# Loading the first x tile alone and transposing the second by DMA in a gated attention/SwiGLU kernel

## The chip, the cores and the metric

The kernel runs on one core of a Trainium2 chip. The metric is the device time of one execution in microseconds (us). The core's engines run side by side: PE (the tensor engine: matmuls, and weight loads shown as PEld), DVE (vector), ACT (scalar), POOL (GpSimd) and SP (sync, which here only issues DMAs). Work on different engines is ordered by semaphores.

## The reference

x has 2048 rows of 512 bf16 values. Two blocks read the same x, and a gate per row mixes them:

```python
g = _sigmoid((x * gate_w).sum(-1, keepdims=True))
a = _A_ref(x, A_wqkv, A_wo)     # linear attention, 32 heads of 16
b = _B_ref(x, B_w1, B_w3, B_w2) # silu(x w1) * (x w3), then w2; inner width 1376
return g * a + (1 - g) * b
```

In block A, `phi(t) = where(t > 0, t + 1, exp(t)) + 1e-6` is applied to q and k; `kv` is the sum over all rows of phi(k) times v per head, `z` the sum of phi(k), and the output is `(phi(q) kv) / (phi(q) z)` times `wo`.

## The kernel before

Rows are worked in 16 tiles of 128 (`t`), the inner dimension of 512 in 4 chunks of 128 (`kc`). Two forms of x are kept on the chip: `xN`, with a row per partition (the natural rows), and `xT`, with a column of x per partition, which the projections need as the stationary operand.

There are two stages. In the first, for each tile, k = x wk and q = x wq are computed (four matmuls of 512 columns each, L169), phi is applied by ACT and DVE, and G, the product of x transposed and phi(k), is summed over all tiles in four PSUM banks (`g_step`, L217), so that v never has to be formed. POOL sums phi(k) for z. In the second stage the SwiGLU matmuls run in blocks of 512 rows, with attention's remaining steps and the output in between. Schedule and queues are written out by hand: each engine runs its instructions in the order of the program.

Nearly all loads are issued by SP on one queue, in the order of the program: the natural rows of tiles 0 and 1 together (L119, 256 KB, with two neighbouring rows of x on one partition, so that "tile 0" holds the even rows of the first 256), the four pieces of wq and wk (`load_wqk`, L116, one piece of 256 KB per `kc`), x tile by tile in transposed form by a transposing DMA for tiles 2 to 15 (`load_xT`, L113), with natural rows in between (L131: tiles 2 and 3 after x tile 3, tiles 4 to 7 after 5, tiles 8 to 15 after 8), and then the other weights. `touch` (L123) is a small load on ACT's queue.

Tiles 0 and 1 get their xT on the tensor engine: `transpose_block` (L323) multiplies a block of xN by the identity into PSUM, and DVE or ACT copies it to xT (L337 to L340, L352). Before that, `warm_step` (L317) runs matmuls on constants. The order on the tensor engine at the start is: 13 warm steps; transposes of chunks 0, 1 and 2 of both tiles (6); the projections of both tiles for kc 0 in the order k0, q0, k1, q1; the 2 transposes of chunk 3; the four projections for kc 1; then k of both tiles for kc 2 and 3, q of tile 0 and of tile 1 for kc 2 and 3, k of tile 2, and three of the four chunks of G of tile 0. Because row pairs were loaded for tiles 0 and 1, their output rows are stored with a stride of two rows.

Of the kernel before, what the change touches and what calls it, by code (L numbers as in the profile page):

```python
# [8 lines left out]
ACT = mybir.ActivationFunctionType  # L9
# [7 lines left out]
def kernel(  # L17
# [17 lines left out]
    nc = tc.nc  # L35
    P = nc.NUM_PARTITIONS
# [5 lines left out]
    KC = D // P  # L42
# [11 lines left out]
    x2d = A_x.flatten_outer_dims()  # L54
    out2d = out.flatten_outer_dims()
# [19 lines left out]
        out=bmask[:], in_=bmask[:], pattern=[[-Dh, HPC], [0, Dh]], compare_op=ALU.is_ge,  # L75
# [3 lines left out]
        out=bmask[:], in_=bmask[:], pattern=[[Dh, HPC], [0, Dh]], compare_op=ALU.is_ge,  # L79
# [17 lines left out]
    xN = consts.tile([P, NT, D], BF16, name="xN")  # L97
# [9 lines left out]
    xT = consts.tile([P, KC, S], BF16, name="xT")  # L107
    act_pre = consts.tile([P, 1], BF16, name="act_pre")
    dq = nc.sync

    def load_xT(t):
        ts = slice(t * P, (t + 1) * P)
        dq.dma_start(out=xT[:, :, ts], in_=x2d[ts, :], transpose=True)  # L113

    def load_wqk(kc):
        dq.dma_start(out=wqk[:, kc, :], in_=wqkv_r[:, kc, 0 : 2 * D])  # L116

    x_first = x2d[0 : 2 * P, :].rearrange("(p j) d -> p j d", j=2)
    dq.dma_start(out=xN[:, 0:2, :], in_=x_first)  # L119
    nc.scalar.activation(out=act_pre[:], in_=warm[:, 0:1], func=ACT.Exp)  # L120

    touch = consts.tile([P, 2, 16], BF16, name="touch")
    nc.scalar.dma_start(out=touch[:], in_=wqkv_r[:, 1:3, 0:16])  # L123
    for kc in range(KC):
        load_wqk(kc)
    natural = {3: (2, 4), 5: (4, 8), 8: (8, 16)}
    for t in range(2, NT):
        load_xT(t)
        if t in natural:
# [2 lines left out]
    with nc.allow_non_contiguous_dma(reason="gate column"):  # L132
        dq.dma_start(
            out=wr[:, :, 2 * FR : NR], in_=gate_w.rearrange("(kc d o) -> d kc o", d=P, o=1)
# [21 lines left out]
    bank = [psum.tile([P, D], FP32, name=f"bank{i}") for i in range(8)]  # L156
    turn = {"mm": 0, "ab": 0}

    def mm_tile():
        turn["mm"] += 1  # L160
        return bank[4 + (turn["mm"] - 1) % 4]

    def ab_tile():
        turn["ab"] += 1
        return bank[(turn["ab"] - 1) % 4]
# [149 lines left out]
    def warm_step(n):  # L315
        for _ in range(n):
            nc.tensor.matmul(  # L317
                bank[7][:, 0:256], lhsT=warm[:, 0:P], rhs=warm, start=True, stop=True
            )

    def transpose_block(t, kc, dst):

        nc.tensor.matmul(  # L323
            dst, lhsT=xN[:, t, kc * P : (kc + 1) * P], rhs=ident[:], start=True, stop=True
        )

    def transpose_kc(kc, ps):
        for t in range(2):
            transpose_block(t, kc, ps[:, t * P : (t + 1) * P])

    warm_step(13)

    for t in range(2):
        transpose_block(t, 0, bank[t][:, 0:P])
    transpose_kc(1, bank[2])
    transpose_kc(2, bank[3])
    nc.vector.tensor_copy(out=xT[:, 0, 0:P], in_=bank[0][:, 0:P])  # L337
    nc.scalar.activation(out=xT[:, 0, P : 2 * P], in_=bank[1][:, 0:P], func=ACT.Copy)
    nc.vector.tensor_copy(out=xT[:, 1, 0 : 2 * P], in_=bank[2][:, 0 : 2 * P])
    nc.scalar.activation(out=xT[:, 2, 0 : 2 * P], in_=bank[3][:, 0 : 2 * P], func=ACT.Copy)  # L340
    first = {(t, n): mm_tile() for n, t in (("k", 0), ("k", 1), ("q", 0), ("q", 1))}
    w_of = {"k": wk, "q": wq}

    def first_mm(n, t, kc):
        proj_mm(first[t, n], t, w_of[n], kc)

    for kc in range(2):
        for n, t in (("k", 0), ("q", 0), ("k", 1), ("q", 1)):
            first_mm(n, t, kc)
        if kc == 0:  # L350
            transpose_kc(3, bank[0])
            nc.vector.tensor_copy(out=xT[:, 3, 0 : 2 * P], in_=bank[0][:, 0 : 2 * P])  # L352
    for kc in range(2, KC):
        for t in range(2):
            first_mm("k", t, kc)
# [67 lines left out]
    def out_step(tb, tt):  # L423
        t = tb * TPB + tt
        ts = slice(t * P, (t + 1) * P)
        tl = slice(tt * P, (tt + 1) * P)
        a_ps = ab_tile()
        for c in range(KC):
            nc.tensor.matmul(  # L429
                a_ps[:], lhsT=pqT[:, c, ts], rhs=M2[:, c, :],  # L430
                start=(c == 0), stop=(c == KC - 1),
            )
        aga = work.tile([P, D], FP32, tag="aga", name="aga")
        nc.scalar.activation(out=aga[:], in_=a_ps[:], func=ACT.Copy, scale=g_all[:, t : t + 1])  # L434
        o = work.tile([P, D], BF16, tag="o", bufs=3, name="o")
        last = t == NT - 1
        for lo, w in ((0, 2 * P), (2 * P, P), (3 * P, P)) if last else ((0, D),):
            cs = slice(lo, lo + w)
            b_ps = ab_tile()
            for fc in range(FC + 1):  # L440
                n = P if fc < FC else FR
                nc.tensor.matmul(  # L442
                    b_ps[:, 0:w], lhsT=hT[tb][:n, fc, tl], rhs=w2[:n, fc, cs],
                    start=(fc == 0), stop=(fc == FC),
                )
            nc.vector.scalar_tensor_tensor(  # L446
                out=o[:, cs], in0=b_ps[:, 0:w], scalar=omg_all[:, t : t + 1], in1=aga[:, cs],
                op0=ALU.mult, op1=ALU.add,
            )
            if t < 2:  # L450
                rows = out2d[0 : 2 * P, :].rearrange("(p j) d -> p j d", j=2)[:, t, :]
            else:
                rows = out2d[ts, :]
            if last and w == P:

                if lo + w < D:
                    continue
                cs = slice(2 * P, D)
            dq.dma_start(out=rows[:, cs], in_=o[:, cs])
# [3 lines left out]
    for tb in range(NTB):  # L463
        for fc in range(FC):
            glu_step(tb, fc)
            if tb == 0:
                if fc in den_at:
                    den_step(den_at[fc])
                if fc == 2:
                    kv_step()  # L470
                if fc == 4:
                    m2_step()
                    z_order()
                    den_products(0)
                if fc == 7:
                    rem_step(0)
        for tt in range(TPB):
            out_step(tb, tt)
            if tb + 1 < NTB:
                if tt == 0:  # L480
                    hT[tb + 1] = work.tile([P, FC + 1, TB], BF16, tag="hT", name="hT")
                if tt == 1:
                    rem_step(tb + 1)
                den_step((tb + 1) * TPB + tt)
# [30 lines left out]
```

## Time and profile before

| what | value |
|---|---|
| median of 3 runs | 179.36 us (178.71 to 179.49) |
| profiled execution, span from first to last instruction | 177.9 us |
| the median less that span | about 1.4 us |
| PE busy | 174.3 us (98%) |
| DVE / ACT / POOL busy | 101.5 / 62.2 / 63.5 us |
| transposes on PE (L323) | 8 matmuls, 6 from 3.74 us and 2 from 6.17 us |
| first projection (L169) starts | 4.51 us |

The profiled execution's time is known by its span; what lies around the span is taken from the difference to the runs. A row of the timeline names the start, the length, the engine, the line, the operation, the tile written and the tile read, and in brackets how long the engine was idle before it and what ended that. SPq is SP issuing a DMA: the length is that of the issue, not of the transfer. Matmuls are pipelined and their ends are modelled, so the distance between starts tells more than the lengths.

### The profile page before, as it was taken

The numbers are of one execution on the slowest core, as the hardware profiler recorded it, in microseconds if no ns is written. First come the engines' busy times: TensorE is split into PE (matmuls) and PEld (weight loads), VectorE is DVE, ScalarE is ACT, GpSimd is POOL, SyncE is SP. The second block draws the span as 40 slices with busy tenths as digits, with TensorE's granted clock in tenths as the row PEclk, the third lists the DMA queues.
The fourth block names the chain that finished last, engine by engine and source line by source line (L and its number), as shares of the span: only waits on it lengthen the run. The fifth ranks groups of instructions, "written<-read, shape, count | busy, mean of one in ns | idle before, by whom it ended". The sixth has DMA issues, their size and how long they took to land.

```text
span 177.9 us, 2504 instructions
## 1 busy us (share of the span) xinstructions
PE 174.3 (98%) x879; PEld 84.1 (47%) x879; DVE 101.5 (57%) x195; ACT 62.2 (35%) x113; POOL 63.5 (36%) x105
## 2 busy tenths in 40 slices
PE   8999999999999999999999999999999999999993
PEld 5444444444454464644444464444445444444453
DVE  0299798888865888666344166634325564333222
ACT  3255444544744332331333223242321223342130
POOL 5077667557301676846300044540004432000000
DMA  6978959993103025243100013520000342000001
GB/s 175 266 209 233 168 100 315 391 350 111 33 0 29 0 55 66 66 95 106 29 0 4 0 33 85 94 57 4 0 0 29 88 92 59 0 0 0 29 33 59
DMA packets 29724, 15.41 MB, mean 87 GB/s; under 512 B 21552, under 2 KB 28048, under 8 KB 29712
## 3 DMA queue, kind: packets, MB, share of 16 engines
q1 hardware_dynamic: 29440, 15.25, 35.2%
q8 instruction: 7, 0.11, 0.3%
q10 hardware_dynamic: 272, 0.01, 0.1%
q14 instruction: 5, 0.04, 0.1%
HBM read 8.56 MB, written 2.10 MB: 60 GB/s over the span
## 4 chain that ended last, share of the span: by engine, by line
PE 98%; DVE 0%; issue 0%
PE bank L442 21%; PE bank L264 19%; PE bank L270 19%; PE bank L169 16%; PE bank L429 8%; PE bank L217 8%; PE bank L231 3%; PE bank L317 2%; PE bank L323 1%; PE bank L404 1%; PE bank L417 0%; DVE o L446 0%
## 5 line engine op out<-in xcount | busy, mean ns | idle before, releaser
L276 DVE TENSOR_TENSOR hT<-bank,sg 128x512 bf16<-128x512 f32 x40 | 27.3, 682 | 32.4 <-PE bank L270 32.4
L264 PE MATMUL bank<-xT,w 128*128 128x512 bf16 x160 | 41.1, 379 | 0.0
L270 PE MATMUL bank<-xT,w 128*128 128x512 bf16 x160 | 41.1, 379 | 0.0
L442 PE MATMUL bank<-w,hT 128*128 128x512 bf16 (+3 forms) x198 | 40.7, 355 | 0.0
L275 ACT ACTIVATE sg<-bank 128x512 bf16<-128x512 f32 x40 | 23.9, 597 | 46.7 <-PE bank L264 46.7
L298 POOL TENSOR_TENSOR pqs<-pq,rden 128x512 bf16<-128x512 bf16 x16 | 16.9, 1056 | 55.7 <-issue 48.2
L169 PE MATMUL bank<-wqk,xT 128*128 128x512 bf16 x128 | 31.2, 386 | 0.0
L442 PEld LDWEIGHTS <-hT 128*128 128x128 bf16 (+1 forms) x198 | 18.5, 98 | 19.8
L446 DVE SCALAR_TENSOR_TENSOR o<-bank,omg_all,aga 128x512 bf16<-128x512 f32 (+2 forms) x18 | 12.4, 692 | 25.6 <-PE bank L442 25.5
L201 POOL TENSOR_TENSOR zacc<-zacc,pk 128x128 f32<-128x128 f32 x56 | 23.3, 446 | 10.4 <-DVE pk L187 10.4
L270 PEld LDWEIGHTS <-w 128*128 128x128 bf16 x160 | 15.7, 98 | 18.9
L264 PEld LDWEIGHTS <-w 128*128 128x128 bf16 x160 | 15.6, 98 | 18.4
L434 ACT ACTIVATE aga<-bank,g_all 128x512 f32<-128x512 f32 x16 | 11.0, 688 | 28.9 <-PE bank L429 28.9
L169 PEld LDWEIGHTS <-xT 128*128 128x128 bf16 x128 | 12.6, 99 | 15.1 <-issue 0.6
L283 POOL TENSOR_TENSOR pr<-pq,zb 128x512 f32<-128x512 bf16 x16 | 18.5, 1156 | 0.1
L217 PE MATMUL bank<-pk,xN 128*128 128x512 bf16 x64 | 16.4, 379 | 0.0
L429 PE MATMUL bank<-M,pqT 128*128 128x512 bf16 x64 | 16.4, 378 | 0.0
L182 ACT ACTIVATE eq<-bank 128x512 bf16<-128x512 f32 x16 | 9.4, 598 | 16.0 <-PE bank L169 16.0
L187 DVE SCALAR_TENSOR_TENSOR pk<-bank,emk 128x512 bf16<-128x512 f32 x16 | 11.1, 692 | 1.6
L182 ACT ACTIVATE ek<-bank 128x512 bf16<-128x512 f32 x16 | 9.5, 597 | 7.1 <-PE bank L169 7.1
L187 DVE SCALAR_TENSOR_TENSOR pq<-bank,emq 128x512 bf16<-128x512 f32 x16 | 11.1, 692 | 0.5
L287 DVE TENSOR_REDUCE den<-pr 128x32 f32<-128x512 f32 x16 | 10.8, 676 | 0.0
(48 smaller groups left out, 82.6 us busy)
## 6 DMA issues: line engine op xcount, KB each, us to landing
w<-in_B_w_dram SPq DMA_DIRECT2D x3, 1280.0 KB, 10.1
out_dram<-o SPq DMA_DIRECT2D x15, 128.0 KB, 1.9
wqk<-in_A_wqkv_dram SPq DMA_DIRECT2D x4, 256.0 KB, 3.9
xN<-in_A_x_dram SPq DMA_DIRECT2D x1, 1024.0 KB, 5.8
xN<-in_A_x_dram SPq DMA_DIRECT2D x2, 256.0 KB, 3.1
xN<-in_A_x_dram SPq DMA_DIRECT2D x1, 512.0 KB, 3.7
wv<-in_A_wqkv_dram SPq DMA_DIRECT2D x1, 512.0 KB, 11.0
wo<-in_A_wo_dram SPq DMA_DIRECT2D x1, 512.0 KB, 12.0
```

Source lines behind the costliest of these rows:

```text
L169: nc.tensor.matmul(ps[:], lhsT=xT[:, kc, t * P : (t + 1) * P], rhs=w[:, kc, :], start=(kc == 0), stop=(kc == KC - 1),)
L182: nc.scalar.activation(out=e[:], in_=ps[:], func=ACT.Exp)
L187: nc.vector.scalar_tensor_tensor(out=dst, in0=ps[:], scalar=0.0, in1=em[:], op0=ALU.max, op1=ALU.add)
L201: nc.gpsimd.tensor_tensor(out=(zaccb if t == NT - 1 else zacc)[:, cs], in0=zacc[:, cs], in1=pk[t][:, cs], op=ALU.add,)
L217: nc.tensor.matmul(bank[kc][:], lhsT=xN[:, t, kc * P : (kc + 1) * P], rhs=pk[t][:], start=(t == 0), stop=(t == NT - 1),)
L264: nc.tensor.matmul(g_ps[:], lhsT=w1[:, kc, fs], rhs=xT[:, kc, tok], start=(kc == 0), stop=(kc == KC - 1),)
L270: nc.tensor.matmul(u_ps[:], lhsT=w3[:, kc, fs], rhs=xT[:, kc, tok], start=(kc == 0), stop=(kc == KC - 1),)
L275: nc.scalar.activation(out=sg[:], in_=g_ps[:], func=ACT.Silu)
L276: nc.vector.tensor_tensor(out=hT[tb][:, fc, :], in0=u_ps[:], in1=sg[:], op=ALU.mult)
L283: nc.gpsimd.tensor_tensor(out=pr[t][:], in0=pq[:, t, :], in1=zb[:], op=ALU.mult)
L429: nc.tensor.matmul(a_ps[:], lhsT=pqT[:, c, ts], rhs=M2[:, c, :], start=(c == 0), stop=(c == KC - 1),)
L442: nc.tensor.matmul(b_ps[:, 0:w], lhsT=hT[tb][:n, fc, tl], rhs=w2[:n, fc, cs], start=(fc == 0), stop=(fc == FC),)
```

## The change

Natural rows of tile 0 are loaded alone (128 KB). x tile 1 comes by a transposing DMA, issued on SP's queue right behind piece 0 of wq/wk and ahead of pieces 1 to 3. Its natural rows are loaded together with those of tiles 2 and 3. The tensor engine runs 12 warm steps instead of 13, transposes only the four chunks of tile 0, each copied at once by DVE or ACT, and the two transposes between kc 0 and kc 1 are gone. Tiles 0 and 1 hold plain rows now, so their stores are like all others.

```diff
-    x_first = x2d[0 : 2 * P, :].rearrange("(p j) d -> p j d", j=2)
-    dq.dma_start(out=xN[:, 0:2, :], in_=x_first)
+    dq.dma_start(out=xN[:, 0, :], in_=x2d[0:P, :])
...
     for kc in range(KC):
         load_wqk(kc)
-    natural = {3: (2, 4), 5: (4, 8), 8: (8, 16)}
+        if kc == 0:
+            load_xT(1)
+    natural = {3: (1, 4), 5: (4, 8), 8: (8, 16)}
...
-    def transpose_kc(kc, ps):
-        for t in range(2):
-            transpose_block(t, kc, ps[:, t * P : (t + 1) * P])
-
-    warm_step(13)
-
-    for t in range(2):
-        transpose_block(t, 0, bank[t][:, 0:P])
-    transpose_kc(1, bank[2])
-    transpose_kc(2, bank[3])
-    nc.vector.tensor_copy(out=xT[:, 0, 0:P], in_=bank[0][:, 0:P])
-    nc.scalar.activation(out=xT[:, 0, P : 2 * P], in_=bank[1][:, 0:P], func=ACT.Copy)
-    nc.vector.tensor_copy(out=xT[:, 1, 0 : 2 * P], in_=bank[2][:, 0 : 2 * P])
-    nc.scalar.activation(out=xT[:, 2, 0 : 2 * P], in_=bank[3][:, 0 : 2 * P], func=ACT.Copy)
+    warm_step(12)
+
+    for kc in range(KC):
+        transpose_block(0, kc, bank[kc][:, 0:P])
+        if kc % 2 == 0:
+            nc.vector.tensor_copy(out=xT[:, kc, 0:P], in_=bank[kc][:, 0:P])
+        else:
+            nc.scalar.activation(out=xT[:, kc, 0:P], in_=bank[kc][:, 0:P], func=ACT.Copy)
...
     for kc in range(2):
         for n, t in (("k", 0), ("q", 0), ("k", 1), ("q", 1)):
             first_mm(n, t, kc)
-        if kc == 0:
-            transpose_kc(3, bank[0])
-            nc.vector.tensor_copy(out=xT[:, 3, 0 : 2 * P], in_=bank[0][:, 0 : 2 * P])
...
-            if t < 2:
-                rows = out2d[0 : 2 * P, :].rearrange("(p j) d -> p j d", j=2)[:, t, :]
-            else:
-                rows = out2d[ts, :]
+            rows = out2d[ts, :]
```

## The prediction

> **What bounds the kernel now.** I read four views in this order. First the page's span, engines and chain:
>
> ```profile
> span 177.9 us, 2504 instructions
> PE 174.3 (98%) x879; PEld 84.1 (47%) x879; DVE 101.5 (57%) x195; ACT 62.2 (35%) x113; POOL 63.5 (36%) x105
> PE 98%; DVE 0%; issue 0%
> ```
>
> The chain that ends last is the tensor engine from end to end. So the change, which touches only the first ten microseconds, counts by how far it moves the point from which that engine runs without a gap: a shift there goes through to the end one for one. The page calls the engine busy nearly everywhere, so stalls must be read from starts. The timeline of the first 10 us (start, length, engine, line):
>
> ```profile
> 0.81 0.40 SPq L119 DMA_DIRECT2D xN<-in_A_x_dram  x1
> 0.84 2.93 PE L317 MATMUL bank<-const-bfloat16-1.0 128*128 128x256 bf16 x13 [0.84 <-PEq L499]
> 1.27 1.83 SPq L116 DMA_DIRECT2D wqk<-in_A_wqkv_dram  x4
> 3.14 2.60 SPq L113 DMA_TRANSPOSE xT<-in_A_x_dram  x2
> 3.74 0.82 PE L323 MATMUL bank<-ident,xN 128*128 128x128 bf16 x6
> 4.07 0.29 DVE L337 CAST xT<-bank 128x128 bf16<-128x128 f32 x1 [4.07 <-PE bank L323]
> 4.51 1.85 PE L169 MATMUL bank<-wqk,xT 128*128 128x512 bf16 x4
> 5.79 0.58 SPq L131 DMA_DIRECT2D xN<-in_A_x_dram  x1
> 6.17 0.30 PE L323 MATMUL bank<-ident,xN 128*128 128x128 bf16 x2
> 6.31 3.62 PE L169 MATMUL bank<-wqk,xT 128*128 128x512 bf16 x16
> ```
>
> Four 512-column matmuls take from 4.51 to 6.17, 0.427 apart; the next sixteen go 0.216 apart. The column of granted clock says 1.00 throughout; the spacing says half speed until about 6.2. SP spends 0.46 on a plain load but 1.3 on a transposing one. Next, the DMA view in narrow windows, one transfer at a time; the last number is us from issue to landing. In order: xN, the four pieces of wqk, x tile 2, and x tile 15, which has the queue to itself:
>
> ```profile
> xN<-in_A_x_dram SPq DMA_DIRECT2D x1, 256.0 KB, 2.9
> wqk<-in_A_wqkv_dram SPq DMA_DIRECT2D x1, 256.0 KB, 3.2
> wqk<-in_A_wqkv_dram SPq DMA_DIRECT2D x1, 256.0 KB, 3.4
> wqk<-in_A_wqkv_dram SPq DMA_DIRECT2D x1, 256.0 KB, 4.4
> wqk<-in_A_wqkv_dram SPq DMA_DIRECT2D x1, 256.0 KB, 4.6
> xT<-in_A_x_dram SPq DMA_TRANSPOSE x1, 4.7
> xT<-in_A_x_dram SPq DMA_TRANSPOSE x1, 2.6
> ```
>
> Issued at 0.81, 1.27, 1.73, 2.20, 2.67 and 3.14, these land at 3.71, 4.47, 5.13, 6.60, 7.27 and 7.84. The transposes start at 3.74 and the first projection at 4.51: each starts as its load lands. The later pieces have room: piece 1 is first used at 6.31, piece 2 at 7.17, piece 3 at 7.17+2x0.216 = 7.60, with 1.2, 0.6 and 0.3 to spare. Last, the table of stretches (columns: PE, PEld, DVE, ACT, POOL busy, clock, DMA share, GB/s) and the packets from 5.85 to 6.65:
>
> ```profile
> 3.10:5.80 2.70, 2.70 (x14) 1.27 (x12) 0.72 (x2) 0.66 (x2) 0.18 (x1) 1.00 1.03 357
> 24.00:24.40 0.40, 0.40 (x3) 0.20 (x2) 0.30 (x1) 0.37 (x1) 0.00 (x0) 1.00 1.07 248
> DMA packets 541, 0.18 MB, mean 224 GB/s; under 512 B 513, under 2 KB 513, under 8 KB 541
> ```
>
> Plain loads run at 357 GB/s, x tile 15's transposing load at 248. By 6.65 the 512 small packets of tile 2 have moved, yet piece 3, ahead of it in the queue, lands only at 7.27 and tile 2 at 7.84.
>
> **The change, part by part.** All against the profiled execution, span 177.93; the median of the runs, 179.36, lies 1.43 above it, and I carry that over unchanged.
>
> *Half the first load.* 128 KB less at 357 GB/s is 0.37: xN lands near 3.34. Twelve warm steps 0.213 apart (the thirteenth of before started at 3.36) end their slots at 3.40. Four transposes 0.107 apart (128 of the 512 columns that take 0.427) follow, to 3.83; copies take 0.29 each, two on DVE and two on ACT, starting 0.33 after the first transpose, so the first piece of xT is ready at 4.02. Transposes are off the path so far.
>
> *Piece 0 of wqk.* Its issue stays at 1.27; with 128 KB less ahead it could land at 4.47-0.37 = 4.10. But it now has a transposing load right behind it, as piece 3 had, and that one's notice came 0.6 after tile 2's packets had moved. Tile 1's packets should move from about 3.1 (its issue ends at 3.0) to 3.9, at most 4.3; so the upper end is 4.9. I take the middle, 4.5: no gain, no loss.
>
> *Tile 1 by DMA.* Issue 1.73 to 3.0. Alone such a load lands 2.6 after issue (4.33); behind the full queue 4.7 (6.43). Only 384 KB stand ahead of it, so I lean to the free row: 4.4 to 5.2. The two matmuls of tile 0 at 4.5 cover it to 4.5+2x0.427 = 5.35. Cost nothing; without that cover up to 1.1.
>
> *Two transposes and a copy between kc 0 and kc 1 go.* 6.17 to 6.31: 0.14 saved. Four cold matmuls from 4.5 end at 6.21; kc 1 starts there, 0.10 ahead of before. Piece 1 must be there: issued at 3.02 instead of 1.73, it lands at 3.02+2.9 (xN's row) = 5.9, at most 5.13+1.29 = 6.42. About covered.
>
> *Pieces 1 to 3 are issued 1.29 later.* This is the cost. Piece 3 is wanted at 6.21+6x0.216 = 7.50. Lower end: the bytes ahead are the same, only tile 1's 128 KB move at 248 instead of 357, +0.16: 7.43, no wait. Upper end: the whole 1.29, 8.56. Between: the plain load issued behind tile 5's transpose ended its issue at 9.54 and reached full rate about 10.6; piece 1, whose issue ends at 3.45, by the same step runs fully at 4.2 to 4.5, and three pieces at 0.75 each end at 6.5 to 6.8 against about 6.2 before. I take +0.5: piece 3 lands at 7.77 and kc 3 of k waits 0.27. Order on the engine keeps all q matmuls behind that wait, so all of it is on the path.
>
> One page bears on this: the Trainium skill, Advanced Engine Details and Errata, X-Bar Transpose (TRN2), says transposing DMAs are as fast as regular ones. The rows here disagree (248 against 357 GB/s, 1.3 against 0.46 of issue); by the page piece 3 would be in time and the sum -0.10.
>
> *Later rows.* Tile 1's rows move to the load after x tile 3: issue at 5.79+1.29 = 7.08, landing 3.3 later plus 0.37 for 128 KB more: 10.75; first used by G of tile 1 at 11.27 plus the shift. Covered with 0.5; without cover, the excess. x tile 2 lands at 7.84+0.5 = 8.34, at worst (1.29) 9.13, and is wanted at 8.90+0.17 = 9.07: covered, at worst 0.06 late. x tile 3 (8.3 before, at worst 9.6) is wanted at 10.41, tile 4 (10.0, 11.3) at 13.2. Everything behind on SP is 1.29 later: the last weights are issued by 37 before and first wanted past 47. The first two stores write plain rows: same bytes, no row waits on them. DVE and ACT lose three copies beside the path.
>
> Sum: -0.10 + 0.27 = +0.17, span 178.1, time 179.53; I say 179.6, since every unread term (hold, second gap) leans to later.
>
> **The rivals.**
> *A, nothing is late.* Pieces 0 and 3 land at their lower ends, 4.10 and 7.43. Then kc 0 ends at 5.81, kc 1 starts 0.4 early with one slow matmul, kc 3 waits at most 0.1: about -0.3, 179.0; if the clock also rises earlier, -0.65, 178.7. For it: equal bytes. Against it: SP's 1.3.
> *B, the queue loses the whole issue.* Piece 3 lands at 8.56 plus up to 0.3 of hold; kc 3 starts 0.95 to 1.25 later than 7.60: 180.3 to 180.6. It decides once piece 3 lands after 8.5. For it: piece 3 lands 0.6 to 1 after its packets. Against it: DMA engines, not SP, were the limit before.
> *C, the slow spell lasts longer.* The slow spacing lasted from 0.84 to 6.2, 5.4 us with gaps of 0.17 and 0.15. Now the gap between transposes and first projection is 0.3 to 1.0. If the count starts anew at 4.5, full speed comes at 9.9: from 6.21 to 9.9 there is room for 3.7/0.427 = 8.7 matmuls, each 0.211 dearer, 1.8 in all, and piece 3's wait vanishes in it: 179.36-0.10+1.83 = 181.1. It decides at a gap long enough to break the count; no row tells how long. The Trainium skill, TensorE: Matmul & The Clock Gate, Part 1, says full clock follows a busy window of about 3.4 us whose phase is free; by it a spoiled window costs about 1.7. The trace agrees on a slow start and shows nothing of the windows.
>
> **How the numbers follow.** Main course (-0.2 to +0.6, 179.2 to 180.0) 0.55; A 0.17; B 0.15; C 0.13. 0.5% is 0.9 us, about what a measurement of this kernel can tell from no change. Faster by that needs all of A and an earlier clock: 0.05. Slower by that: B and C, 0.28. Within: 0.67. The range runs from just below A's end to B's end, 178.6 to 180.8; C (0.13) and A's tail stay outside.
>
> **What would show it.** Right: transposes at 3.4, first projection about 4.5, no L323 row after kc 0, a gap of 0.2 to 0.5 on the tensor engine before kc 3 (near 7.5), piece 3 landing 7.5 to 8.0, G steps without a gap. Wrong: first projection at 4.1 and no gap (A); piece 3 after 8.5 (B); 0.427 spacing beyond 6.5 (C); a gap in front of G of tile 1 if its rows land after 11.4.

## The result, and the profile after

| | kernel before | changed kernel |
|---|---|---|
| median of 14 runs each | 179.35 us (178.70 to 179.78) | 180.05 us (179.61 to 180.33) |
| ratio to before | | 1.0041, interval 1.0029 to 1.0054 |
| profiled execution | span 177.9 | span 178.2, time 180.05 |

Medians, ranges and numbers of runs, here and below, are those of executions at the usual speed; single slower ones, of 1.5% and more above the fastest of their kernel, are left out.

The change costs 0.70 us between the medians. That is inside the prediction's 0.5%, but near its slow end and just above the main course, which ended at 180.0. The interval lies wholly above 1, so the loss is clear of the noise.

The page of the changed kernel, its span, its busy times and, from its fourth part, the chain that ended last by engine:

```profile
span 178.2 us, 2478 instructions
...
PE 172.7 (97%) x858; PEld 83.6 (47%) x874; DVE 100.9 (57%) x194; ACT 62.0 (35%) x113; POOL 63.4 (36%) x105
...
PE 94%; DMA 2%; SPq 2%; issue 1%; DVE 0%
```

PE's busy time fell by 1.6, but the 21 matmuls that are missing against the 879 of before are only in part gone (four transposes and a warm step); the others are most likely missing records: a second profile of the unchanged kernel, with 863, lacks the same 16. More telling, the chain is no longer PE alone: 2% of it is a DMA and 2% SP's issues. The chain in order of time says where (start, length, what):

```profile
1.73 1.29 SPq L113
...
3.06 0.57 SPq L116
...
3.68 0.43 SPq L116
...
4.15 3.59 DMA wqk<-in_A_wqkv_dram
7.75 0.04 issue
7.79 2.32 PE bank L170 x10
```

SP's time goes straight into the chain: the transposing load of tile 1 holds SP for 1.29, so piece 3 of wq/wk is issued at 4.15 (before: 2.67), lands at 7.75, and the tensor engine, which wanted it earlier, starts kc 3 at 7.79. From there to the end the chain is PE again. The timeline of the same stretch (start, length, engine, line; in brackets the idle time before and what ended it):

```profile
3.36 0.63 PE L324 MATMUL bank<-ident,xN 128*128 128x128 bf16 x4
4.40 1.28 PE L170 MATMUL bank<-wqk,xT 128*128 128x512 bf16 x4 [0.41 <-DMA wqk<-in_A_wqkv_dram]
5.07 0.33 PEld L170 LDWEIGHTS <-xT 128*128 128x128 bf16 x3 [0.56 <-DMA xT<-in_A_x_dram]
5.97 4.14 PE L170 MATMUL bank<-wqk,xT 128*128 128x512 bf16 x16 [0.29 <-DMA wqk<-in_A_wqkv_dram]
```

The row at 5.97 hides two more gaps, because it joins sixteen matmuls. The single starts of the 512-column matmuls, taken from the traces, show them (`|` marks a gap):

```
after    4.40 4.78 5.07 5.30 | 5.97 6.19 6.40 6.62 | 7.08 7.30 | 7.79 8.00 ...  G of tile 0 at 9.94
before   4.51 4.89 5.32 5.75 | 6.31 6.52 6.74 6.96   7.17 7.39   7.60 7.82 ...  G of tile 0 at 9.76
```

In before's row the mark stands for the two transposes there. Full speed (0.216 from start to start) came at 4.8 in this execution and at 6.2 in before's. So the tensor engine was through with each piece sooner, and waited three times, by the starts less 0.216: 0.46 before kc 1, 0.25 before kc 2, 0.28 before kc 3. It all ends where piece 3 lands. The DMA view, one transfer at a time, gives tile 1's transposing load and pieces 1, 2 and 3, in this order (the last number is us from issue to landing; the issues are at 1.73, 3.06, 3.68 and 4.15):

```profile
xT<-in_A_x_dram SPq DMA_TRANSPOSE x1, 3.3
wqk<-in_A_wqkv_dram SPq DMA_DIRECT2D x1, 256.0 KB, 2.9
wqk<-in_A_wqkv_dram SPq DMA_DIRECT2D x1, 256.0 KB, 3.4
wqk<-in_A_wqkv_dram SPq DMA_DIRECT2D x1, 256.0 KB, 3.6
```

Each piece is faster from issue to landing than before (3.4, 4.4 and 4.6 there), with less of the queue still ahead of it; but it is issued 1.33 to 1.48 later, and that is not won back in full: they land at 5.93, 7.04 and 7.75 instead of 5.13, 6.59 and 7.27. The stretch from 4.0 to 5.5 in the table of stretches, first of the changed kernel, then of the one before (last two columns: share of the DMA engines, GB/s):

```profile
4.00:5.50 1.50, 1.10 (x4) 0.42 (x5) 0.21 (x2) 0.31 (x2) 0.00 (x0) 1.00 0.83 207
```

```profile
4.00:5.50 1.50, 1.50 (x9) 0.81 (x7) 0.72 (x2) 0.66 (x2) 0.00 (x0) 1.00 1.01 348
```

The transfers that before kept the queue full run at 207 GB/s in a stretch where before moved 348. That hole goes with the later issue; whether it alone makes it is taken up below.

From about 8 us on, PE has no gap in either kernel. So the effect on the tensor engine is in the start: in the two profiled executions G of tile 0 begins at 9.76 and 9.94 (+0.18). Another 0.10 lies behind the last matmul, where the span goes on for 2.80 in before and 2.90 after. Together that is 0.28 of the 0.70. The rest is taken up below.

The 0.10 has nothing to do with the pieces. The changed kernel has one DMA more (73 against 72). At the end SP waits for the semaphores of the DMAs one after another; when the last store has landed, one such wait is left in before, and in the changed kernel the one that SP stands at and two more. The kernels of the experiments show the same: from the end of the last matmul to the end of the span it is 2.79 to 2.80 in the six traces with 72 DMAs, 2.88 to 2.90 in the seven with 73, and 3.04 in the one with 75.

### The profile page after: what moved, and what is told of

It reads as the page before. It is cut to its first block, busy times and chain, and to the rows that moved or that the text cites. A ratio compares the mean times of both kernels' runs of the same rounds, so it can differ in the third digit from the quotient of the medians.

```text
span 178.2 us, 2478 instructions
## 1 busy us (share of the span) xinstructions
PE 172.7 (97%) x858; PEld 83.6 (47%) x874; DVE 100.9 (57%) x194; ACT 62.0 (35%) x113; POOL 63.4 (36%) x105
## 4 chain that ended last, share of the span: by engine, by line
PE 94%; DMA 2%; SPq 2%; issue 1%; DVE 0%
PE bank L434 21%; PE bank L265 20%; PE bank L271 19%; PE bank L170 14%; PE bank L421 8%; PE bank L218 8%; PE bank L232 3%; DMA wqk<-in_A_wqkv_dram 2%; SPq L116 1%; SPq L113 1%; PE bank L396 1%; PE bank L409 0%; SPq L118 0%; DVE o L438 0%
## 5 line engine op out<-in xcount | busy, mean ns | idle before, releaser
L265 PE MATMUL bank<-xT,w 128*128 128x512 bf16 x158 | 41.0, 379 | 0.3
L434 PE MATMUL bank<-w,hT 128*128 128x512 bf16 (+4 forms) x197 | 40.6, 355 | 0.1
L271 PE MATMUL bank<-xT,w 128*128 128x512 bf16 x154 | 40.3, 379 | 0.2
```

What stands on the lines that cost most here:

```text
L265: nc.tensor.matmul(g_ps[:], lhsT=w1[:, kc, fs], rhs=xT[:, kc, tok], start=(kc == 0), stop=(kc == KC - 1),)
L271: nc.tensor.matmul(u_ps[:], lhsT=w3[:, kc, fs], rhs=xT[:, kc, tok], start=(kc == 0), stop=(kc == KC - 1),)
L434: nc.tensor.matmul(b_ps[:, 0:w], lhsT=hT[tb][:n, fc, tl], rhs=w2[:n, fc, cs], start=(fc == 0), stop=(fc == FC),)
```

## The experiments

The theory on which the expectations rest ("Theory 1" in some of them): the pieces are issued late because SP spends 1.29 on a transposing load, and the tensor engine waits for them; the profiled execution of before stands above its own median, so the loss seen against it is too small. The rivals: the place of the transposing load in the queue, not SP's time, holds the pieces; the gaps keep the matmul clock low for longer; or something else in the start than the pieces. Medians are given with the number of runs; the kernel before, run beside them in three groups, had 179.34, 179.44 and 179.32 us.

| kernel | median us (range, runs) | ratio, interval | KB moved by 5.5 us | piece 3 lands |
|---|---|---|---|---|
| before, again | 179.35 (178.74-179.96, 12) | 1.0004 [0.9988, 1.0020] | 1108 | 7.22 |
| before, a third time | 179.53 (1) | | 1122 | 6.76 |
| before, plain rows behind piece 3 | 179.33 (178.79-179.78, 12) | 0.9992 [0.9978, 1.0006] | 1094 | 6.61 |
| before, first load split | 179.80 (179.19-181.49, 12) | 1.0036 [1.0012, 1.0060] | 906 | 7.37 |
| before, one tiny load | 180.06 (179.59-180.50, 7) | 1.0038 [1.0022, 1.0054] | 856 | 7.23 |
| before, three tiny loads | 180.09 (179.80-180.28, 12) | 1.0031 [1.0018, 1.0043] | 816 | 7.48 |
| before, wk first | 180.24 (179.72-181.80, 10) | 1.0064 [1.0037, 1.0090] | 849 | other pieces |
| before, no warm steps | 180.75 (179.55-182.19, 11) | 1.0069 [1.0041, 1.0097] | 1008 | 7.05 |
| after, tile 1 by a plain load | 180.22 (179.83-182.08, 10) | 1.0061 [1.0032, 1.0090] | 826 | 7.80 |
| after, three warm steps more | 180.16 (179.97-180.34, 10) | 1.0042 [1.0029, 1.0054] | 754 | 7.92 |
| after, pieces on ACT's queue | 181.16 (180.55-182.73, 6) | 1.0115 [1.0075, 1.0154] | 766 | 9.01 |
| after, no warm steps | 181.15 (180.83-181.94, 6) | 1.0102 [1.0077, 1.0126] | 698 | 7.59 |

The ratios are to the kernel before. The column of KB is the sum of the data packets that ended by 5.5 us in the profiled execution; in before's own trace it is 1074, in the changed kernel's 774. The last two columns are of one execution each; piece 3's landing went from 6.76 to 7.27 between three executions of the unchanged kernel alone.

### The kernel before once more

No edit. The question was what an undisturbed execution's span stands for.

> The kernel before, unchanged, for the spans and a second profiled execution. Theory 1: what lies around a span is about 1.74 us, as in the executions of the changed kernel (180.05 against 178.3), so the profiled execution of before (span 177.93) stood for about 179.67, 0.3 above its median, and executions in which the tensor engine reaches full speed earlier than 6.2 us have spans down to 177.0; piece 3 lands near 7.3 in all of them. Rival: about 1.43 lies around the span before and the missing 0.4 us of the measured difference arise later in the kernel; then the spans here lie at 177.9 in the middle.

Measured: 179.35, and a profiled execution of 179.66 with a span of 177.9. Time less span was 1.66 to 1.88 in the executions of both kernels, 1.74 in the mean, so the 1.43 of the rival does not occur. The profiled execution of before, span 177.93, therefore stood for about 177.93 + 1.75 = 179.68, which only two of its 14 runs exceed, and not for the median. A median execution of before has a span of 177.6 (in these twelve the spans went from 176.9 to 178.2); the changed kernel's went from 177.9 to 178.6, and its profiled execution is its median. So against the median the span grew by 0.6, and the +0.28 between the two profiles is only the part that these two executions show.

### Tile 1 by a plain load, transposed on the tensor engine

```diff
         if kc == 0:
-            load_xT(1)
-    natural = {3: (1, 4), 5: (4, 8), 8: (8, 16)}
+            dq.dma_start(out=xN[:, 1, :], in_=x2d[P : 2 * P, :])
+    natural = {3: (2, 4), 5: (4, 8), 8: (8, 16)}
...
+    for t in range(2):
+        for kc in range(2):
+            for n in ("k", "q"):
+                first_mm(n, t, kc)
+            if t == 0 and kc == 0:
+                transpose_tile(1)
```

> As after, but tile 1's x is loaded as natural rows by a plain load behind piece 0 and transposed on the tensor engine. Theory 1 (the transposing load's issue of 1.29 us ahead of pieces 1 to 3 is the cost): pieces 1 to 3 are issued 0.46 later than before instead of 1.3 to 1.5, piece 3 lands at 7.3 to 7.5, time 179.2 to 179.6, so most of the 0.7 us is back. Rival (loading the first tile alone, one warm step less, or separate copies cost it): stays at 180.0.

A miss: 180.22, no better than the change. SP lost only 0.47 in front of piece 1, issued at 2.19 (3.06 in the changed kernel); yet it landed at 6.50, 0.57 later than there. The timeline of this kernel:

```profile
6.54 4.04 PE L170 MATMUL bank<-wqk,xT 128*128 128x512 bf16 x18 [1.57 <-DMA wqk<-in_A_wqkv_dram]
```

The tensor engine waited 1.57 for kc 1 in one piece, and the order k0, q0 of kc 0 left it only two matmuls and four transposes to fill that time. The table of stretches of this kernel:

```profile
4.00:5.50 1.50, 0.92 (x6) 0.49 (x7) 0.70 (x3) 0.75 (x4) 0.00 (x0) 1.00 0.89 198
```

The hole in the transfers is there without a transposing load in front of the pieces, as deep as in the changed kernel (207). So a transposing load's 1.29 on SP is not needed for the loss. The run removes that issue but not cleanly: the changed order of the matmuls has its part in the 1.57, and the rival of the expectation, that loading the first tile alone costs something, is not separated from it.

### The three pieces on ACT's queue

```diff
-        dq.dma_start(out=wqk[:, kc, :], in_=wqkv_r[:, kc, 0 : 2 * D])
+        (dq if kc == 0 else nc.scalar).dma_start(out=wqk[:, kc, :], in_=wqkv_r[:, kc, 0 : 2 * D])
```

> As after, but pieces 1 to 3 of wq/wk are issued on ACT's queue behind the small touch load, so they no longer wait for SP's issue of tile 1's transposing load; bytes and transposes are the same. Theory 1 (SP's issue): piece 3 lands at 7.0 to 7.4, the gaps on the tensor engine before kc 1 to kc 3 shrink, time 179.3 to 179.7. Rival (it is the transposing load in the DMA engines, by its slower packets and by what it holds back, and not its issue): piece 3 still lands after 7.6 and the time stays within 0.15 of 180.05.

A miss by 1.5: 181.16. Two rows of its timeline:

```profile
5.74 2.59 PE L170 MATMUL bank<-wqk,xT 128*128 128x512 bf16 x10 [1.75 <-DMA wqk<-in_A_wqkv_dram]
9.05 2.32 PE L170 MATMUL bank<-wqk,xT 128*128 128x512 bf16 x10 [0.72 <-DMA wqk<-in_A_wqkv_dram]
```

Piece 0, the only piece left on SP's queue, now landed at 5.70 instead of 4.36, and piece 3 at 9.01. The run isn't a clean removal of SP's delay: with the pieces gone from its queue SP issues the transposing loads of tiles 2 and 3 at 3.06 and 4.36, among the pieces, and the two queues share the 16 DMA engines. It tells nothing on the theory, only that a second queue in this form is no way out. The Trainium skill, DMA: Bandwidth & Descriptors, "Issuing engines are not separate DMA queues", says that starting DMAs from several engines saves no more than the issuing time, as they interleave on the same engines. This run agrees: with loads of both queues in flight together, piece 0 took 4.43 from issue to landing instead of 3.09, more than the queue's own issue could save.

### Before, with a plain load behind piece 3

```diff
         load_wqk(kc)
-    natural = {3: (2, 4), 5: (4, 8), 8: (8, 16)}
+    dq.dma_start(out=xN[:, 2:4, :], in_=x_t[:, 2:4, :])
+    natural = {5: (4, 8), 8: (8, 16)}
```

> The kernel before, with the natural rows of tiles 2 and 3 issued right behind piece 3 and x tile 2's transposing load after them. Theory 1 (a transposing load right behind holds back the landing of the load ahead of it): piece 3 lands at 6.5 to 6.9 instead of 7.27, x tile 2 at about 8.6, wanted at 8.9; time 179.0 to 179.3, lower only in executions with an early full clock. Rival (piece 3 lands when its own data are through): it lands at 7.1 to 7.3 as before, and the time is the same or, if tile 2 comes late, up to 0.3 higher.

This asks whether a transposing load holds the landing of the plain load in front of it. Piece 3 in this kernel, by the DMA view:

```profile
wqk<-in_A_wqkv_dram SPq DMA_DIRECT2D x1, 256.0 KB, 3.9
```

It took 3.9 from issue to landing, against 4.6 in before's trace with a transposing load behind it: 6.61 instead of 7.27, as expected. But that does not show a hold. In the third trace of before, with the transposing load behind it, piece 3 landed at 6.76. And the landing followed the piece's own data in both orders: it came 0.40 behind the last 2 KB packet of the pieces in before, 0.39 and 0.40 in its second and third trace, and 0.41 here. What differs is when that last packet ended: at 6.87, 6.83 and 6.36 in the traces of before, and at 6.20 here. In before's trace the last of them come one by one, 0.08 apart, while 28 small packets beside them took 0.47 to 0.87 us and ended at 7.06 to 7.10; here three took over 0.25. So a transposing load may slow the last packets in some executions; that it holds the notice is not shown.

The time is the same, 0.9992 with an interval that reaches 0.9978. In the profiled execution full speed came only at 6.6, and then piece 3 is not wanted before 7.75.

### Before, with small loads behind piece 0

The issue delay by itself, with before's order on the tensor engine and its first load untouched: three loads of 4 KB that nobody reads, then only one.

```diff
+    tiny = consts.tile([P, 3, 16], BF16, name="tiny")
     for kc in range(KC):
         load_wqk(kc)
+        if kc == 0:
+            for i in range(3):
+                dq.dma_start(out=tiny[:, i, :], in_=wqkv_r[:, 3, 16 * i : 16 * i + 16])
```

> The kernel before with three tiny plain loads (4 KB each, never used) behind piece 0: SP's issue of pieces 1 to 3 and all that follows is 1.3 to 1.4 us later, as in the changed kernel, but no transposing load and no bytes to speak of stand in between. Theory 1 (SP's issue time is the cost): piece 3 lands at 7.6 to 8.0, the tensor engine waits for pieces 1 to 3, time 179.9 to 180.2, as after. Rival 2 (the transposing load in the DMA engines is the cost; its issue is hidden behind the queue's backlog): piece 3 lands within 0.2 of 7.27, time 179.3 to 179.6.

180.09: 0.65 above the kernel before, nearly as much as the change's loss, from nothing but 12 KB in three loads. Of this 0.25 lies behind the last matmul, in the three DMAs more that SP waits for at the end; the change has 0.10 there. The chain of this kernel:

```profile
4.09 3.39 DMA wqk<-in_A_wqkv_dram
...
7.52 2.32 PE bank L173 x10
```

And two rows of its timeline:

```profile
5.84 1.46 PE L173 MATMUL bank<-wqk,xT 128*128 128x512 bf16 x6 [0.31 <-DMA wqk<-in_A_wqkv_dram]
7.52 2.32 PE L173 MATMUL bank<-wqk,xT 128*128 128x512 bf16 x10 [0.23 <-DMA wqk<-in_A_wqkv_dram]
```

The picture is that of the changed kernel: piece 3 issued at 4.09, and PE, at full speed from about 3.9, waits for the pieces. One reservation: this profiled execution is one of the two fastest of its twelve (179.80), and G of tile 0 starts in it at 9.68, no later than in before's own trace. The time shows the loss; the trace shows the waits for the pieces, but not how much of the loss they make.

With one small load instead of three, SP's delay is 0.47:

> The kernel before with one tiny plain load (4 KB, never used) behind piece 0 instead of three: pieces 1 to 3 are issued 0.47 us later. Theory 1 (the cost grows with the delay of the issue beyond what the backlog of the queue hides): piece 3 lands at 7.0 to 7.5, time between before and the run with three tiny loads, 179.5 to 179.8. Rival (half a microsecond is hidden by the backlog): 179.3 to 179.5.

A miss: 180.06, as much as with three, or 0.65 and 0.40 more than before when the part behind the last matmul (0.09 and 0.25) is taken off. The cost does not grow with the delay, which speaks against SP's time as the measure of it. The profiled execution (179.68, the second lowest of seven) had full speed only at 6.2, and no wait at all:

```profile
6.26 3.62 PE L172 MATMUL bank<-wqk,xT 128*128 128x512 bf16 x16
```

Its table of stretches, and below it that of the kernel with three small loads:

```profile
4.00:5.50 1.50, 1.50 (x8) 0.74 (x7) 0.72 (x2) 0.66 (x2) 0.00 (x0) 1.00 0.80 233
```

```profile
4.00:5.50 1.50, 1.38 (x11) 0.73 (x9) 0.63 (x2) 0.63 (x2) 0.00 (x0) 1.00 0.80 217
```

One load of 4 KB goes with nearly the same hole: 233 GB/s against 348. Yet in this execution the hole did little harm: the pieces landed at 5.91, 6.53 and 7.23 against 5.13, 6.59 and 7.27 in before's trace, only piece 1 later, and that one was not wanted before 6.26. So the loss of 0.74 stands in the runs, and the trace shows only the 0.09 at the end of it.

What goes with the loss over these kernels is not how long SP was held but that the stream of large plain loads was broken: in the table above the kernels with warm steps and a whole stream have moved 1074 to 1122 KB by 5.5 us, and their medians are 179.3 to 179.4; those with an extra or an otherwise cut load have moved 754 to 906 and take 179.8 or more. That is a thing that goes along with the loss, not a cause shown, and why one small load does it stays open.

### The first load in two halves

```diff
-    x_first = x2d[0 : 2 * P, :].rearrange("(p j) d -> p j d", j=2)
-    dq.dma_start(out=xN[:, 0:2, :], in_=x_first)
+    for t in range(2):
+        dq.dma_start(out=xN[:, t, :], in_=x2d[t * P : (t + 1) * P, :])
```

> The kernel before with the first load of 256 KB cut into the plain rows of tile 0 and of tile 1, 128 KB each, both ahead of piece 0; all pieces are issued 0.46 later. Theory 1: as with one tiny load, 179.5 to 179.8. Rival (loads with rows of 1 KB leave a hole in the transfers behind them, which is what the run with the plain second tile suffered): 180.0 to 180.3, with a stretch of under 200 GB/s between 4.4 and 5.8 us.

179.80 (0.48 more), at the upper edge of what was expected. Piece 0 lands at 4.80 instead of 4.47, as its issue moves by one load, and the tensor engine waits for it:

```profile
4.84 1.02 PE L169 MATMUL bank<-wqk,xT 128*128 128x512 bf16 x4 [0.43 <-DMA wqk<-in_A_wqkv_dram]
```

One more load in front of the pieces costs something even where the bytes are the same; 0.10 of it lies behind the last matmul. This execution (179.54) is also the nearest to a before with an early clock: full speed was there by 4.8, piece 3 landed at 7.37, and G of tile 0 started at 9.56, earlier than in any of the three traces of before.

### wk ahead of wq

Before, with the wk halves in front (kc 0, then kc 1 to 3), then wq in two loads, and all k projections of both tiles first.

```diff
-    for kc in range(KC):
-        load_wqk(kc)
+    for a, b, c in ((0, 1, D), (1, KC, D), (0, 2, 0), (2, KC, 0)):
+        dq.dma_start(out=wqk[:, a:b, c : c + D], in_=wqkv_r[:, a:b, c : c + D])
```

> The kernel before with wk's halves of the pieces loaded first (kc 0, then kc 1 to 3) and wq's in two loads behind, and the k projections of all four kc ahead of those of q. If the landing of the last piece sets the pace in executions with an early full clock, only four matmuls instead of six come after it and k's phi starts earlier: 179.0 to 179.3. If the tensor engine's own slow start sets the pace in most executions: 179.3 to 179.5.

A miss: 180.24. The second load (384 KB, issued at 1.73) landed at 6.37 as a whole, and until then the tensor engine had only kc 0:

```profile
6.41 4.05 PE L169 MATMUL bank<-wqk,xT 128*128 128x512 bf16 x18 [1.17 <-DMA wqk<-in_A_wqkv_dram]
```

Pieces of one kc each were the better cut here: work can start as each lands.

### The clock: three warm steps more, and none

The prediction's rival C held that a gap in the tensor engine's work makes the slow spell longer. Three warm steps behind the four transposes fill the gap before the first projection.

```diff
+    warm_step(3)
     first = {(t, n): mm_tile() for n, t in (("k", 0), ("k", 1), ("q", 0), ("q", 1))}
```

> The changed kernel with three more warm steps (0.64 us at half speed) behind the four transposes, in the gap in which the tensor engine waits for piece 0. Theory 1: no change, 179.9 to 180.2, since piece 3 sets the pace. Rival 4 (the new gaps keep the tensor engine slow for longer in some executions): faster by 0.2 to 0.5.

180.16, no change. Its timeline:

```profile
4.19 1.17 PE L170 MATMUL bank<-wqk,xT 128*128 128x512 bf16 x4
6.07 1.02 PE L170 MATMUL bank<-wqk,xT 128*128 128x512 bf16 x4 [0.71 <-DMA wqk<-in_A_wqkv_dram]
```

Full speed was there by 4.2, the gap before kc 1 grew to 0.71 (0.29 in the changed kernel's row), and piece 3 set the end again (7.92). The rival falls: filling the gap gave nothing back. Rival C had fallen before that: in the changed kernel's own trace the slow spacing ended at 4.8, and none of its 14 runs is above 180.33.

Then without any warm step, in the kernel before (`warm_step(13)` taken out) and in the changed one (`warm_step(12)` taken out), so that the clock rises late in both and PE's own slowness covers the late pieces:

> The kernel before without its 13 warm steps, so that the tensor engine is at half speed well beyond 7 us and needs pieces 1 to 3 later than they land. All theories: slower than before, 180.3 to 181.5. It is the reference for the next run.

> The changed kernel without its 12 warm steps. Theory 1 (the loss is the tensor engine, already at full speed, waiting for late pieces): at half speed the pieces are in time, piece 3 is wanted only near 8.7, and the change no longer costs: 0.4 below to 0.1 above before without warm steps. Rival 3 (the change costs something that doesn't hang on the pieces, further down): 0.5 to 0.9 above it, as with warm steps.

180.75 and 181.15. At half speed until about 9.4 and 10.3 the pieces are hardly missed any more; of the changed kernel's waits for pieces 1 to 3 only the one before kc 1 is left:

```profile
6.24 5.62 PE L170 MATMUL bank<-wqk,xT 128*128 128x512 bf16 x16 [0.24 <-DMA wqk<-in_A_wqkv_dram]
```

kc 3 of k starts at 8.87 before and at 8.75 after: up to there the changed kernel is ahead by 0.12, as the theory says for a clock that rises late. But G of tile 0 starts at 11.30 and 11.69, since full speed came 0.9 later in the second execution, and the runs of before without warm steps spread over 2.6 us. So the difference of the medians, +0.40, can't be told from none; it lies between what the theory and its rival expected, and the pair decides nothing.

### The kernel before a third time

No edit. The question was whether an execution of before with an early clock has a short span.

> The kernel before, unchanged, for one more profiled execution. Its span should follow the moment at which the 512-column matmuls go from 0.427 to 0.216: for each microsecond earlier than 6.2 the span is 0.5 shorter, down to where piece 3's landing is the limit; 176.9 to 178.2. Rival: the span varies with something else, and a short span goes with a late full clock.

179.53, span 177.8, and again half speed until 6.2, so the question stays open. Its timeline:

```profile
4.62 1.64 PE L169 MATMUL bank<-wqk,xT 128*128 128x512 bf16 x4 [0.20 <-DMA wqk<-in_A_wqkv_dram]
6.21 3.62 PE L169 MATMUL bank<-wqk,xT 128*128 128x512 bf16 x16
```

Like the other two it lies above before's median; an execution of before that is as short as its median was not caught. Piece 3 landed at 6.76 in it, half a microsecond before the other two (7.27 and 7.22): its landing is not fixed by the order of the loads, and the expectation of the first repetition, near 7.3 in all, does not hold.

## Why the prediction was right, and where it was not

The prediction said 179.6 with 0.67 for "within 0.5%" and a range from 178.6 to 180.8. The time is 180.05. The steps one by one:

- *Half the first load*: right where it counts. xN landed at 3.02, 0.32 earlier than was said, but the warm steps set the transposes' start: 3.36 against 3.40.
- *Piece 0*: right within 0.14. It landed at 4.36, between the bounds of 4.10 and 4.9. The upper bound rests on a misreading: by 6.65 only 482 of tile 2's 512 small packets had ended in before's trace, the other 30 ended by 7.10, and piece 3's landing came 0.40 behind its own last packet. No run shows a hold of 0.6.
- *Tile 1 by DMA*: right. It landed at 5.03 (4.4 to 5.2 was said), 3.3 after its issue. PE's first two matmuls of tile 0 covered it but for less than 0.1: the weight load at 5.07 in the timeline above waited for it. Slow matmuls would have covered it better than these did.
- *Two transposes gone, 0.10 saved, and piece 1 "about covered"*: this failed in its working. It supposed four cold matmuls until 6.21. In the profiled execution full speed came at 4.8, kc 0 was done at 5.5, and piece 1 (5.93, said 5.9) and piece 2 (7.04) were both waited for. It made no difference to the end of this execution, since piece 3 decides.
- *Pieces 1 to 3 issued 1.29 later, piece 3 at 7.77, a wait of 0.27 before kc 3*: right in the numbers, in part by luck. It landed at 7.75; the wait was 0.28. The middle value taken, +0.5, measured +0.48. But the +0.5 was chosen between 0.16 and 1.29, the landing of piece 3 differs by 0.5 between executions of the unchanged kernel alone, and the wait was to come behind four slow matmuls, where it came behind faster ones and two other waits. Where the row and the Trainium skill's sentence on the speed of transposing DMAs (Advanced Engine Details and Errata, X-Bar Transpose (TRN2)) were weighed, piece 3 was late as by the row, and the load held SP for 1.29; but with a plain load in its place piece 3 was as late (7.80), so this does not decide between the two.
- *Later rows*: right. Tile 1's natural rows landed at 10.70 (10.75), x tile 2 at 8.30 (8.34), x tile 3 at 8.84; PE shows no gap behind kc 3.
- *The sum, +0.17 on the span*: against the profiled execution right. G of tile 0 starts 0.18 later, the span is 178.2 (178.1). The 0.10 that one DMA more costs behind the last matmul was not in the sum.
- *"The median of the runs, 179.36, lies 1.43 above it, and I carry that over unchanged"*: this is the step that failed, and it makes most of the miss of 0.45. Time less span is about 1.75, so before's profiled execution was one of its longer ones (179.68), and 0.32 too little was added. With 1.75 the same sum gives 178.1 + 1.75 = 179.85; of the remaining 0.2, 0.10 lies behind the last matmul, and the changed kernel's profiled execution has 1.84 between span and time. In other words, against before's median the change cost 0.70 and not the 0.17 of the sum or the 0.24 that was said.

What the step missed can perhaps be put so: the price of the late pieces depends on when the clock rises. With full speed only at 6.2, as in before's profile, before wants piece 3 at 7.60 and the change's 7.75 costs little. If full speed came at 4.5 in before, the same landings (5.13, 6.60, 7.27) would let it start kc 3 at about 7.31, 0.29 earlier, which takes 179.68 to 179.39, close to its median. The changed kernel can't use an early clock, as it must wait until 7.75. Four traces with an early clock fit this: in the changed kernel, in the same with its gap filled, and in before with the first load split and with three tiny loads, G of tile 0 starts 2.20 behind piece 3's landing (at 7.75, 7.92, 7.37 and 7.48). For before itself it is argued from landing times: no trace of it with an early clock was caught, and the kernel with plain rows behind piece 3, which landed at 6.61 and should then gain more, gained nothing that could be measured. So the split of the 0.70 into 0.28 that the two profiles show and 0.4 that only the medians show is measured, and the cause of the 0.4 stays open.

The rivals: A (nothing late) did not occur: piece 3 landed at 7.75, not 7.43, with equal bytes. B (piece 3 past 8.5) did not occur. C did not occur (the slow spacing ended at 4.8), and filling the gap gave nothing. That SP's issue time is the cause, the prediction's reading, holds in part: a pure delay with three small loads gives nearly the same loss, but one small load costs as much, and a plain load in place of the transposing one does not give it back. What is shown is that every version with warm steps and a load more on SP's queue, ahead of the pieces or between them, cost 0.5 to 0.9 as long as the pieces stayed on that queue, of which 0.1 (0.25 with three loads) lies behind the last matmul; that it is SP's 1.29 in particular is not.

Not tried: tile 1's transposing load on ACT's queue, and the change with tile 1 behind piece 3 and tile 0 worked alone until then. No version that was run is faster than the kernel before; the one with plain rows behind piece 3 can't be told from it.

## What to carry to other kernels

Find out what a profiled execution stands for before a sum is made against it: time less span, measured on any execution that has both, tells whether the profile is of a median run, and here that was a larger error than all the steps of the sum together. A load moved ahead of others can cost more than its own bytes, the landing of everything behind it, so look for the last of a run of loads that the bound engine waits for and price the move there. An engine that is slow at the start hides late transfers, so price them also for the case in which it isn't slow. And count the DMAs: each one more made this kernel's end longer by 0.08 to 0.10.

## What the runs showed of the hardware

- One plain load of 4 KB behind the first of four large ones went with transfers of 233 instead of 348 GB/s between 4.0 and 5.5 us, and the kernel took 180.06 instead of 179.32 us. Three of them cost no more (180.09).
- A load's landing came 0.39 to 0.41 behind its own last packet, whether the load behind it was a transposing one (three traces of before) or a plain one; the last packet itself ended anywhere from 6.36 to 6.87 in the unchanged kernel.
- One DMA more lengthened the time from the last matmul to the end of the span from 2.79-2.80 to 2.88-2.90 us, three more to 3.04, as SP waits for their semaphores one after another.
- Three pieces on a second queue landed later, the last at 9.01 instead of 7.75, and the piece left on the first queue at 5.70 instead of 4.36.
- With warm steps the tensor engine's first matmul is at 0.84 in every trace, but full speed came anywhere from 3.9 to 6.6 us, while the column of granted clock said 1.00 all that time; without warm steps (first matmul at 3.64 and 2.95) it came at 9.4 and 10.3. In ten of the fourteen traces the record of the clock begins only at that moment (4.80 in the changed kernel), and the column shows 1.00 where there is no record.
